# One attention-block backward loop: dO pass in two PSUM banks, dH of Q apart, tail work moved behind pass and fold

## The chip, the cores and the metric

The kernel runs on one core of one Trainium2 chip. The metric is the device time of one execution in microseconds, the median of several runs. A core has TensorE (matrix products and transposes into PSUM[...]), VectorE and ScalarE (both read PSUM and copy it to SBUF, which is called eviction here), GpSimd[...] and SyncE, which here only issues DMAs. Each engine works its instructions in program order and waits on semaphores.

## The reference, cut to what matters

The reference returns a forward pass and the gradients of all its inputs. The forward pass is an attention block with a recurrent memory, then a gated MLP, each behind a modulated layer norm. In the attention block the 2048 rows are 64 segments of 32. Each segment is worked together with 8 memory rows, and its first 8 output rows are the memory of the next segment:

```python
for s in range(n_seg):                                     # 64 segments
    xs = x[:, s * seg_len:(s + 1) * seg_len, :].copy()     # 32 rows
    h = jnp.concatenate([mem, xs], axis=1)                 # 40 rows of 512
    q = jnp.einsum('btd,dhe->bhte', h, Wq)                 # 32 heads of 128
    k = jnp.einsum('btd,dhe->bhte', h, Wk)
    v = jnp.einsum('btd,dhe->bhte', h, Wv)
    scores = jnp.einsum('bhqe,bhke->bhqk', q, k) * scale
    scores = jnp.where(mask[None, None], scores, -1000000000.0)
    p = _softmax(scores, axis=-1)
    o = jnp.einsum('bhqk,bhke->bhqe', p, v)
    o = jnp.einsum('bhte,hed->btd', o, Wo)
    mem = o[:, :M, :].copy()
    outs.append(o[:, M:, :])
...
_out, _vjp = jax.vjp(_f, A_x, A_mem0, A_Wq, A_Wk, A_Wv, A_Wo, B_w_gate, B_w_up, B_w_down, c, w_mod)
_grads = _vjp(grad_out)
```

Backward, the segments run from the last to the first. A step takes the gradient dy of the segment's output (32 rows of which the 8 of the memory come from the step just done), and forms dO = dy Wo^T, dV, dS, dK, dQ per head, and dH = dV Wv^T + dK Wk^T + dQ Wq^T, the gradient of the 40 rows. The 8 memory rows of dH are needed before the next step's dO pass can begin: this is the recurrence.

## The kernel before: the parts that the change touches

Products with few rows use TensorE as four column tiles: a stationary operand of 32 columns fills one tile, and four matmuls with different tiles run side by side. A result of 512 columns thus stands in one bank as four partial rows of 32, which are added up by a "fold": the sum is split into a bf16 high part and a bf16 low part, and short matmuls with a selecting matrix (`foldsel`) add the four quarters and turn them at once.

```python
    row = pool.tile([1, 128], F32, name="modrow", bufs=1)
    nc.scalar.activation(row[:], ps[0:1, :], AF.Copy)
    nc.gpsimd.dma_start(self.MODROW[:, sl], row[:])

return load, products
...

    j = n % 4
    self.nc.tensor.matmul(ps[32 * j:32 * j + 32, :], lhsT=lhsT, rhs=w, start=(n < 4), stop=(n >= total - 4),
                          tile_position=(0, 32 * j))

def pair_mm(self, ps, x, w, n, total):

    nc = self.nc
...
def col_pass(self, psp, w, hf, lhs, rows, eng):

    E, DC = self.cfg.E, self.cfg.DC
    ps = psp.tile([128, 512], F32, name="pass_ps", tag="p")
    for c in range(DC):
        wc = w[:, c, :].rearrange("p (h e) -> p h e", e=E)
        for j in range(4):
            rhs = wc[:, 12 * hf + j:12 * hf + j + 10:3, :] if j < 3 else wc[:, 24 + 4 * hf:28 + 4 * hf, :]
            self.nc.tensor.matmul(ps[32 * j:32 * j + 32, :], lhsT=lhs(c), rhs=rhs, start=(c == 0), stop=(c == DC - 1),
                                  tile_position=(0, 32 * j))
    if eng is None:
        return ps
    self.evac(eng, rows[:, 512 * hf:512 * hf + 512], ps[:])
...
def fold_split(self, pool, ps, name, tags=""):

    nc = self.nc
    parts = []
    for h in range(2):
        sl = slice(256 * h, 256 * h + 256)
        hi = pool.tile([128, 256], BF16, name=name + "_hi", tag=f"{tags}hi{h}", bufs=1)
        nc.scalar.activation(hi[:], ps[:, sl], AF.Copy)
        parts.append(hi)
    for h in range(2):
        lo = pool.tile([128, 256], BF16, name=name + "_lo", tag=f"{tags}lo{h}", bufs=1)
        nc.vector.tensor_tensor(lo[:], ps[:, 256 * h:256 * h + 256], parts[h][:], op=ALU.subtract)
        parts.append(lo)
    return parts

def fold_sum(self, psp, parts, name, tag):

    ft = psp.tile([128, self.cfg.DC, 32], F32, name=name + "_ft", tag=tag)
    for c in range(self.cfg.DC):
        for i in range(2):
            self.nc.tensor.matmul(ft[:, c, :], lhsT=parts[2 * i + c // 2][:, (c % 2) * 128:(c % 2) * 128 + 128],
                                  rhs=self.foldsel[:], start=(i == 0), stop=(i == 1))
    return ft
...
def store_rows(self, psp, pool, ft, dram, name, tag, then=None):

    nc = self.nc
    tb = pool.tile([128, 128], BF16, name=name + "_tb")
    nc.vector.tensor_copy(tb[:], ft[:].rearrange("p c r -> p (c r)"))

    def f():
        tp = psp.tile([128, 128], BF16, name=name + "_tp", tag=tag)
        nc.tensor.transpose(tp[:], tb[:], self.ident[:])
        rb = pool.tile([128, 128], BF16, name=name + "_rb")
        nc.vector.tensor_copy(rb[:], tp[:])
        nc.gpsimd.dma_start(dram, rb[:])
        if then is not None:
            then(rb)

    self.later.append(f)
```

`pair_mm` puts two heads side by side in such a bank: two column tiles take the left, two the right half of the 512 columns, so its result is 256 wide and folds with `foldhalf`. The forward pass uses it; the backward loop does not. In the loop (`NS` = 64 steps, `G` = 11 groups of three heads, 128 columns each, worked in `NP` = 3 parts of 4, 4 and 3 groups) the pools and the parts concerned are:

```python
rxp = ctx.enter_context(tc.tile_pool(name="p4rx", bufs=3, reuse_waits="tile"))
sb2 = ctx.enter_context(tc.tile_pool(name="p4s2", bufs=2, reuse_waits="tile"))
psp = ctx.enter_context(tc.tile_pool(name="p4ps", bufs=6, space=PSUM, reuse_waits="tile"))
psb = ctx.enter_context(tc.tile_pool(name="p4psb", bufs=1, space=PSUM, reuse_waits="tile"))
...
def turn(hf):
    for k, eng in enumerate(("act", "dve")):
        tp = psp.tile([128, 2, 128], BF16, name="turn_ps", tag="p")
        i0 = 4 * hf + 2 * k
        for i in range(2):
            nc.tensor.transpose(tp[:, i, :], RAd[:, (i0 + i) * 128:(i0 + i + 1) * 128], self.ident[:, :])
        to_heads(eng, tp[:], i0, 2, 0, 32, 0)
...
def proj_b(t, hf):
    ps = self.col_pass(psp, WoT, hf, lambda c: dbs[t][:, c, :, :].rearrange("p s q -> p (s q)"), None, None)
    return lambda: self.evac(("act", "dve")[hf], RBds[t % 2][:, 512 * hf:512 * hf + 512], ps[:])
...
def grad_out(nm, xt, pi, eng, ps):
    self.evac(eng, part3(xt, pi), ps[:, 0:min(PG, G - pi * PG), :])
    if pi == NP - 1:
        rows = rxp.tile([128, G, 128], BF16, name="rows_x")
        nc.sync.dma_start(rows[:], xt[:, :], transpose=True)
        dram = {"dVT": self.DVR, "dKT": self.DKR, "dQT": self.DQR}[nm][s]
        row_stores.append(lambda: nc.gpsimd.dma_start(dram, rows[:]))
...
def dht(X, WT, pi):
    if dh_ps[0] is None:
        dh_ps[0] = psb.tile([128, 512], F32, name="dh_ps", tag="dh")
    for h in range(pi * PG * 3, min(H, (pi + 1) * PG * 3)):
        off = (h // 3) * GW + (h % 3) * 32
        self.col_mm(dh_ps[0], X[:, off:off + 32], WT[:, h, :], n_dh[0], 3 * H)
        n_dh[0] += 1

for hf in range(2):
    self.col_pass(psp, WoT, hf, lambda c: dyT[:, c, :], RAd, ("dve", "act")[hf])
    nc.gpsimd.tensor_copy(dOst[0:96, 512 * hf:512 * hf + 512], RAd[0:96, 512 * hf:512 * hf + 512])
if pend:
    pend.pop()()
store_rows_x(1)
if s == 0:
    self.p5_first()
turn(0)
turn(1)
gv0 = grad_mm("dVT", dOst, Pst, 0)
prod(0)
dp(0)
prod(1)
dp(1)
prod(2)
dp(2)
gv1 = grad_mm("dVT", dOst, Pst, 1)
grad_out("dVT", dVT, 0, "act", gv0)
dost(2)
grad_out("dVT", dVT, 1, "act", gv1)
ds(0)
ds(1)
ds(2)
self.pop_later()
dht(dVT, WvT, 0)
dht(dVT, WvT, 1)
if s > 0:
    to_heads("pool", btd[:], 0, 8, 32, 8, 8 * ((s - 1) % nseg_t))
if s4 == 3 and s > 3:
    get_db(s // 4 - 1)
store_rows_x(0)
if s == 0:
    self.p5_second()
for pi in range(NP):
    dstt(pi)
gks = [grad_mm("dKT", Qst, dS, pi) for pi in range(NP)]
load_rows(Qst_t, self.QST, s - 1)
gv2 = grad_mm("dVT", dOst, Pst, 2)
if s > 0:
    dO_tails(s - 1)
for pi in range(NP):
    grad_out("dKT", dKT, pi, "dve", gks[pi])
grad_out("dVT", dVT, 2, "act", gv2)
self.pop_later()
for pi in range(NP):
    grad_part("dQT", Kst, dST, dQT, pi, "act")
split = tail.split()
load_rows(Kst_t, self.KST, s - 1)
for pi in range(NP):
    dht(dKT, WkT, pi)
dht(dVT, WvT, 2)
if split:
    self.pop_later()
for pi in range(NP):
    dht(dQT, WqT, pi)
parts = self.fold_split(sb2, dh_ps[0], "dh")
tail.collect(s % nseg_t, [dVT, dKT, dQT])
tail.chunk()
ft = self.fold_sum(psp, parts, "dh", "p")
if dyT_next is not None:
    nc.scalar.activation(dyT_next[:, :, 0:M], ft[:, :, 0:M], AF.Copy)
if s > 3:
    if s4 >= 2:
        proj_b(s // 4 - 1, 3 - s4)()
    elif s4 == 1:
        turn_b(s // 4 - 1)()
...
pend.append(lambda ft=ft, s=s, then=then: self.store_rows(psp, sb2, ft, self.DHA[s], "dh", "p", then))
if s4 == 0:
    tail.begin(s, [WvT, WkT, WqT])
```

`turn` transposes dO per head pair and copies it into dOT, which the dp products read; `proj_b` and `turn_b` do the dO pass and its turning for the memory rows of the next group of four segments. The tail (`TailRows`) gathers the last 8 rows of dV, dK and dQ over four segments (`collect`) and forms their dH once a group: 96 matmuls with 32 stationary columns in four pieces of 24, one piece a step (`chunk`); then `split` makes high and low part of the sum, and its fold runs when `pop_later` is next called. `row_stores` hands the turned rows of dK, dV and dQ to GpSimd's DMA queue in that order.

## Time and profile before

| what | value |
|---|---|
| time, median of 3 runs | 3183.44 us (3178.51 to 3185.88) |
| span of the profiled run | 3180.4 us, mean granted TensorE clock 0.983 |
| TensorE, weight load | 2985.1 us (94%), 1729.6 us (54%) |
| VectorE, ScalarE, GpSimd | 1579.3 us (50%), 1161.1 us (37%), 1481.1 us (47%) |
| DMA moved | 726.12 MB, mean 228 GB/s |
| backward loop: first dO pass to the last one | 1570.8 to 2555.5 us |

The profile names an instruction by its engine, its line in the kernel (a helper's line where a helper records it) and by tiles, output left of the arrow. A square bracket holds the idle time of the engine before it and what ended it. PE is TensorE's matmul side, PEld its loading of stationary operands, DVE VectorE, ACT ScalarE, POOL GpSimd and SP SyncE. TensorE's matmuls are pipelined and their ends are modelled, so distances between starts are safer than durations. A busy share over the whole span says little here, as the program has several phases; the loop is read by itself.

### The profile page before, as it was taken

The numbers are of one execution on the slowest core, as the hardware profiler recorded it, in microseconds if no ns is written. First come the engines' busy times: TensorE is split into PE (matmuls) and PEld (weight loads), VectorE is DVE, ScalarE is ACT, GpSimd is POOL, SyncE is SP. The second block draws the span as 40 slices with busy tenths as digits, with TensorE's granted clock in tenths as the row PEclk, the third lists the DMA queues.
The fourth block names the chain that finished last, engine by engine and source line by source line (L and its number), as shares of the span: only waits on it lengthen the run. The fifth ranks groups of instructions, "written<-read, shape, count | busy, mean of one in ns | idle before, by whom it ended". The sixth has DMA issues, their size and how long they took to land.

```text
span 3180.4 us, 98869 instructions
## 1 busy us (share of the span) xinstructions
PE 2985.1 (94%) x40069; PEld 1729.6 (54%) x40069; DVE 1579.3 (50%) x3770; ACT 1161.1 (37%) x2829; POOL 1481.1 (47%) x2973
## 2 busy tenths in 40 slices
PE   5999999999998899989999999999999969999999
PEld 3666666666665444445555555555555534445454
DVE  4655666666654777642245455554554521332221
ACT  2454454454454433322244444444444410100011
POOL 3666666666664466521244444444444421233322
PEclk8999999999999899999999999999999989999999
DMA  8788888889888798897599999999999999998886
GB/s 291 206 208 208 202 201 207 198 206 212 198 206 236 182 221 219 209 294 245 171 260 255 265 256 263 268 274 263 263 261 251 261 226 223 231 213 192 204 231 152
DMA packets 958892, 726.12 MB, mean 228 GB/s; under 512 B 656018, under 2 KB 831138, under 8 KB 958308
## 3 DMA queue, kind: packets, MB, share of 16 engines
q1 hardware_dynamic: 827940, 508.77, 71.1%
q0 software_dynamic: 59056, 148.62, 13.9%
q10 hardware_dynamic: 71440, 62.40, 7.8%
q8 instruction: 316, 5.18, 0.7%
q14 instruction: 140, 1.15, 0.1%
HBM read 294.91 MB, written 276.33 MB: 180 GB/s over the span
## 4 chain that ended last, share of the span: by engine, by line
PE 34%; DMA 9%; issue 8%; ACT 3%; POOL 2%; DVE 2%; SPq 1%; ACTq 0%; POOLq 0%; DVEq 0%
PE dh_ps L212 10%; PE gps L1820 5%; PE pass_ps L249 4%; PE g_ps L1509 4%; PE dh_tps L212 2%; DMA rows<-DKR 2%; PE gps5o L1833 2%; PE tps L1424 2%; PE dp_ps L1488 1%; DMA rows<-DQR 1%; PE dp_ps L1496 1%; ACT RAd L61 1%; DMA rows<-OSR 1%; PE dh_ft L318 1%; PE turn_ps L1390 1%
## 5 line engine op out<-in xcount | busy, mean ns | idle before, releaser
L1820 PE MATMUL gps<-rows,hrows 128*128 128x512 bf16 (+2 forms) x2160 | 417.8, 355 | 4.5 <-ACT ot L61 3.1
L1820 PEld LDWEIGHTS <-hrows 128*128 128x128 bf16 x2160 | 211.1, 98 | 209.4 <-issue 5.1
L249 PEld LDWEIGHTS <-hT 128*32 128x32 bf16 x6144 | 158.2, 97 | 161.3 <-issue 1.9
L1538 POOL COPY dOst<-RAd 96x512 bf16<-96x512 bf16 x128 | 78.6, 614 | 356.4 <-DVE RAd L63 345.0
L852 POOL TENSOR_TENSOR Pst<-Pst,rden 120x1408 bf16<-120x1408 bf16 x63 | 161.2, 2559 | 114.7 <-issue 81.5
L1824 POOL DMA_DIRECT2D out_dram<-ot x108 | 81.5, 755 | 232.9 <-DVE ot L63 138.9
L63 DVE CAST ot<-gps 128x512 bf16<-128x512 f32 (+3 forms) x76 | 47.9, 633 | 254.0 <-PE gps L1820 122.5
L309 DVE TENSOR_TENSOR dh_lo<-dh_ps,dh_hi 128x256 bf16<-128x256 f32 x128 | 48.4, 420 | 240.2 <-ACT dh_hi L305 240.2
L1833 PE MATMUL gps5o<-WoT,rows 128*128 128x512 bf16 x600 | 134.3, 387 | 26.6 <-DMA rows<-OSR 26.6
L61 ACT ACTIVATE ot<-gps 128x512 bf16<-128x512 f32 (+3 forms) x75 | 41.2, 549 | 281.4 <-PE gps L1820 128.7
L212 PE MATMUL dh_ps<-WvT,dVT 128*32 128x512 bf16 x2048 | 136.1, 385 | 0.0
L249 PE MATMUL pass_ps<-Wv,hT 128*32 128x512 bf16 x2048 | 133.5, 380 | 0.0
L1498 DVE SCALAR_TENSOR_TENSOR dS<-dp_ps,Pst_l 128x512 bf16<-128x512 f32 (+1 forms) x192 | 112.2, 640 | 35.0 <-PE dp_ps L1496 34.9
L249 PE MATMUL pass_ps<-WoT,dyT 128*32 128x512 bf16 x2048 | 122.9, 382 | 5.2 <-ACT dyT L1597 5.2
L220 PE MATMUL at_ps<-Wo,OT 128*32 128x256 bf16 x4096 | 124.7, 275 | 0.5 <-DVE OT L63 0.2
L249 PE MATMUL pass_ps<-Wk,hT 128*32 128x512 bf16 x2048 | 123.6, 383 | 1.5 <-ACT hT L842 1.1
L63 DVE CAST RA0v<-pass_ps 128x512 bf16<-128x512 f32 x128 | 88.4, 690 | 70.5 <-PE pass_ps L249 68.1
L212 PE MATMUL dh_ps<-WkT,dKT 128*32 128x512 bf16 x2048 | 122.4, 380 | 0.0
L212 PE MATMUL dh_ps<-WqT,dQT 128*32 128x512 bf16 x2048 | 121.9, 379 | 0.0
L249 PE MATMUL pass_ps<-Wq,hT 128*32 128x512 bf16 x2048 | 121.8, 379 | 0.0
L61 ACT ACTIVATE dVT<-g_ps 128x512 bf16<-128x512 f32 (+1 forms) x192 | 108.1, 563 | 36.6 <-PE g_ps L1509 20.5
L694 ACT ACTIVATE ET<-st_ps 128x480 bf16<-128x480 f32 (+1 forms) x192 | 96.2, 537 | 53.7 <-ACT qT L61 37.0
(411 smaller groups left out, 7035.9 us busy)
## 6 DMA issues: line engine op xcount, KB each, us to landing
OSR<-Ost SPq DMA_DIRECT2D x64, 352.0 KB
OT<-OT SPq DMA_DIRECT2D x64, 352.0 KB
VT<-VTr SPq DMA_DIRECT2D x64, 352.0 KB
PS<-Pst SPq DMA_DIRECT2D x64, 352.0 KB
OT_l<-OT SPq DMA_DIRECT2D x64, 352.0 KB
Pst_l<-PS SPq DMA_DIRECT2D x64, 352.0 KB
VT_l<-VT SPq DMA_DIRECT2D x64, 352.0 KB
DKR<-rows_x POOLq DMA_DIRECT2D x64, 352.0 KB, 5.8
```

The costliest lines, as they stand in the source:

```text
L61: return nc.scalar.activation(out, in_, AF.Copy)
L63: return nc.vector.tensor_copy(out, in_)
L212: self.nc.tensor.matmul(ps[32 * j:32 * j + 32, :], lhsT=lhsT, rhs=w, start=(n < 4), stop=(n >= total - 4), tile_position=(0, 32 * j))
L220: nc.tensor.matmul(ps[32 * j:32 * j + 32, :], lhsT=x[k], rhs=w[k][:, 256 * d:256 * d + 256], start=(n == 0), stop=(n == total - 1), tile_p ...
L249: self.nc.tensor.matmul(ps[32 * j:32 * j + 32, :], lhsT=lhs(c), rhs=rhs, start=(c == 0), stop=(c == DC - 1), tile_position=(0, 32 * j))
L694: nc.scalar.activation(part3(ET, pi)[:, 0:n, 0:120], st_ps[:, 0:n, 0:120], AF.Exp, scale=cfg.scale)
L852: nc.gpsimd.tensor_tensor(Pst[0:120, :, :], Pst[0:120, :, :], rden[:, :].unsqueeze(2).to_broadcast([120, G, 128]), op=ALU.mult)
L1498: nc.vector.scalar_tensor_tensor(out=part3(dS, pi), in0=ps[:, 0:n, :], scalar=cfg.scale, in1=part3(Pst, pi), op0=ALU.mult, op1=ALU.mult)
L1509: nc.tensor.matmul(ps[:, j, :], lhsT=lh[:, g * GW:(g + 1) * GW], rhs=rh[:, g * GW:(g + 1) * GW], start=True, stop=True)
L1820: nc.tensor.matmul(ps[:, 0:ng * E], lhsT=hrows[:, tp_, c * 128:(c + 1) * 128], rhs=rows[:, tp_, 0:ng * E], start=(tp_ == 0), stop=(tp_ == ...
L1824: nc.gpsimd.dma_start(outw[c * 128:(c + 1) * 128, h0:h0 + 3 * (ng - 1) + 1:3, :], ot[:, 0:ng * E].rearrange("p (h e) -> p h e", e=E))
L1833: nc.tensor.matmul(pss[gg][:], lhsT=rows[:, tp_, gg * E:(gg + 1) * E], rhs=dyrows[:, tp_, :], start=(tp_ == order[0]), stop=(tp_ == order[ ...
```

## The change

It reorders the hand-over between two steps of the backward loop and gives some of its results a place of their own:

- the dO pass of a step goes in three pieces (heads groups of 4, 2 and 2 in each column tile) instead of two; the last two have a bank each and are evicted apart by ScalarE;
- dH of V and K alone goes into the bank `dh_ps` and is split while TensorE does dH of Q, which is formed in pairs in a bank of its own; the fold adds both;
- high and low part are 512 wide and live in dST and dS, which are free by then;
- the tail's 96 matmuls go in seven pieces, some behind the dO pass and one behind the fold; its own fold moves next to the step's fold; the memory rows' dO pass uses the bank of `dh_ps`, and half of each of its halves stands behind the fold, the other half behind the next dO pass;
- the transpose of dV into rows is issued in two parts, eight groups early and three late.

It is meant to give TensorE work where it waits for an eviction, and to start one transpose earlier. Cut to its core:

```diff
-    def col_pass(self, psp, w, hf, lhs, rows, eng):
+    def col_pass(self, psp, w, hf, lhs, rows, eng, ps=None, cs=None, steps=None):
 
         E, DC = self.cfg.E, self.cfg.DC
-        ps = psp.tile([128, 512], F32, name="pass_ps", tag="p")
-        for c in range(DC):
+        a, n = steps or (4 * hf, 4)
+        if ps is None:
+            ps = psp.tile([128, n * E], F32, name="pass_ps", tag="p")
+        for c in cs or range(DC):
             wc = w[:, c, :].rearrange("p (h e) -> p h e", e=E)
             for j in range(4):
-                rhs = wc[:, 12 * hf + j:12 * hf + j + 10:3, :] if j < 3 else wc[:, 24 + 4 * hf:28 + 4 * hf, :]
+                rhs = wc[:, 3 * a + j:3 * (a + n - 1) + j + 1:3, :] if j < 3 else wc[:, 24 + a:24 + a + n, :]
                 self.nc.tensor.matmul(ps[32 * j:32 * j + 32, :], lhsT=lhs(c), rhs=rhs, start=(c == 0), stop=(c == DC - 1),
                                       tile_position=(0, 32 * j))
         if eng is None:
             return ps
-        self.evac(eng, rows[:, 512 * hf:512 * hf + 512], ps[:])
+        self.evac(eng, rows[:, a * E:(a + n) * E], ps[:])
...
-    def fold_split(self, pool, ps, name, tags=""):
+    def fold_split(self, pool, ps, name, home=None):
 
         nc = self.nc
...
+        hi, lo = (pool.tile([128, 512], BF16, name=f"{name}_{x}", tag=x, bufs=1)[:, :] if home is None
+                  else home[:, 512 * i:512 * i + 512] for i, x in enumerate(("hi", "lo")))
+        nc.scalar.activation(hi, ps[:], AF.Copy)
+        nc.vector.tensor_tensor(lo, ps[:], hi, op=ALU.subtract)
+        return hi, lo
+
+    def fold_sum(self, psp, parts, name, tag, pair=()):
 
         ft = psp.tile([128, self.cfg.DC, 32], F32, name=name + "_ft", tag=tag)
-        for c in range(self.cfg.DC):
-            for i in range(2):
-                self.nc.tensor.matmul(ft[:, c, :], lhsT=parts[2 * i + c // 2][:, (c % 2) * 128:(c % 2) * 128 + 128],
-                                      rhs=self.foldsel[:], start=(i == 0), stop=(i == 1))
+        cs = range(self.cfg.DC)
+        mms = [(t[:, c * 128:(c + 1) * 128], self.foldsel[:], c) for t in parts for c in cs]
+        mms += [(t[:, (c % 2) * 128:(c % 2) * 128 + 128], self.foldhalf[:, c // 2, :], c) for t in pair for c in cs]
+        for n, (lhsT, rhs, c) in enumerate(mms):
+            self.nc.tensor.matmul(ft[:, c, :], lhsT=lhsT, rhs=rhs, start=(n == 0), stop=(n >= len(mms) - self.cfg.DC),
+                                  skip_group_check=True)
         return ft
...
-def proj_b(t, hf):
-    ps = self.col_pass(psp, WoT, hf, lambda c: dbs[t][:, c, :, :].rearrange("p s q -> p (s q)"), None, None)
-    return lambda: self.evac(("act", "dve")[hf], RBds[t % 2][:, 512 * hf:512 * hf + 512], ps[:])
+def proj_b(t, hf, parts=1):
+    ps = psb.tile([128, 512], F32, name="pass_ps", tag="dh")
+
+    def part(k):
+        self.col_pass(psp, WoT, hf, lambda c: dbs[t][:, c, :, :].rearrange("p s q -> p (s q)"), None, None, ps,
+                      range(k * DC // parts, (k + 1) * DC // parts))
+
+    part(0)
+
+    def rest():
+        for k in range(1, parts):
+            part(k)
+        return lambda: self.evac(("act", "dve")[hf], RBds[t % 2][:, 512 * hf:512 * hf + 512], ps[:])
+
+    return rest
...
-tail = TailRows(self, sb2, psp, psb, 3, "dh", self.DHB, 4)
+b_rest = []
+tail = TailRows(self, sb2, psp, psb, 3, "dh", self.DHB, (16, 24, 8, 8, 16, 8, 16), home=dSs[0])
...
+        early = 2 * PG if nm == "dVT" else 0
+        if pi == 1 and early:
+            turned[nm] = rxp.tile([128, G, 128], BF16, name="rows_x")
+            nc.sync.dma_start(turned[nm][:, 0:early, :], xt[:, 0:early * GW], transpose=True)
         if pi == NP - 1:
-            rows = rxp.tile([128, G, 128], BF16, name="rows_x")
-            nc.sync.dma_start(rows[:], xt[:, :], transpose=True)
+            rows = turned.get(nm) or rxp.tile([128, G, 128], BF16, name="rows_x")
+            nc.sync.dma_start(rows[:, early:G, :], xt[:, early * GW:G * GW], transpose=True)
             dram = {"dVT": self.DVR, "dKT": self.DKR, "dQT": self.DQR}[nm][s]
             row_stores.append(lambda: nc.gpsimd.dma_start(dram, rows[:]))
...
-            self.col_mm(dh_ps[0], X[:, off:off + 32], WT[:, h, :], n_dh[0], 3 * H)
+            self.col_mm(dh_ps[0], X[:, off:off + 32], WT[:, h, :], n_dh[0], 2 * H)
             n_dh[0] += 1
 
+    def dht_pairs(X, WT):
+        ps = psp.tile([128, 256], F32, name="dhq_ps", tag="p")
+        off = lambda h: (h // 3) * GW + (h % 3) * 32
+        for n in range(H // 2):
+            hs = (2 * n, 2 * n + 1)
+            self.pair_mm(ps, [X[:, off(h):off(h) + 32] for h in hs], [WT[:, h, :] for h in hs], n, H // 2)
+        return ps
+
+    for a, n, eng in ((0, 4, "dve"), (4, 2, "act"), (6, 2, "act")):
+        self.col_pass(psp, WoT, 0, lambda c: dyT[:, c, :], RAd, eng, steps=(a, n))
     for hf in range(2):
-        self.col_pass(psp, WoT, hf, lambda c: dyT[:, c, :], RAd, ("dve", "act")[hf])
         nc.gpsimd.tensor_copy(dOst[0:96, 512 * hf:512 * hf + 512], RAd[0:96, 512 * hf:512 * hf + 512])
-    if pend:
-        pend.pop()()
+    b_done = b_rest.pop()() if b_rest else None
+    if s4 < 2:
+        tail.chunk()
     store_rows_x(1)
     if s == 0:
         self.p5_first()
...
     grad_out("dVT", dVT, 0, "act", gv0)
+    if b_done:
+        b_done()
     dost(2)
     grad_out("dVT", dVT, 1, "act", gv1)
...
+    parts = self.fold_split(sb2, dh_ps[0], "dh", dST)
+    pair = self.split_pair(sb2, dht_pairs(dQT, WqT), "dh")
+    tail.collect(s % nseg_t, [dVT, dKT, dQT])
+    tail.chunk()
     if split:
         self.pop_later()
-    for pi in range(NP):
-        dht(dQT, WqT, pi)
-    parts = self.fold_split(sb2, dh_ps[0], "dh")
-    tail.collect(s % nseg_t, [dVT, dKT, dQT])
-    tail.chunk()
-    ft = self.fold_sum(psp, parts, "dh", "p")
+    ft = self.fold_sum(psp, parts, "dh", "p", pair)
     if dyT_next is not None:
         nc.scalar.activation(dyT_next[:, :, 0:M], ft[:, :, 0:M], AF.Copy)
-    if s > 3:
-        if s4 >= 2:
-            proj_b(s // 4 - 1, 3 - s4)()
-        elif s4 == 1:
-            turn_b(s // 4 - 1)()
+    g = s // 4
+    if s >= NS - 2:
+        proj_b(g - 1, 3 - s4)()()
+    elif s4 == 3 and g > 0:
+        b_rest.append(proj_b(g - 1, 1, 2))
+    elif s4 == 2:
+        tail.chunk()
+    elif s4 == 1 and g > 0:
+        turn_b(g - 1)()
+    elif s4 == 0 and g > 1:
+        b_rest.append(proj_b(g - 2, 0, 2))
...
-    pend.append(lambda ft=ft, s=s, then=then: self.store_rows(psp, sb2, ft, self.DHA[s], "dh", "p", then))
+    self.store_rows(psp, sb2, ft, self.DHA[s], "dh", "p", then)
     if s4 == 0:
         tail.begin(s, [WvT, WkT, WqT])
-pend.pop()()
```

## The prediction

> **What bounds the kernel now.** I read the slices of the span first, then busy time by stretch, then the order of TensorE's instructions inside one step of the backward loop, then the waits. The change touches only that loop: 64 steps, whose first dO pass starts at 1570.8 us and whose last stretch ends at about 2570 us, one third of the span. In the middle of it:
>
> ```profile
> core 0: us, PE busy (x) PEld busy (x) DVE busy (x) ACT busy (x) POOL busy (x), PEclk, DMA share, GB/s
> 2000.00:2150.00 150.00, 144.35 (x2442) 86.62 (x2439) 77.70 (x210) 68.93 (x177) 70.25 (x174) 1.00 1.13 269
> ```
>
> TensorE is busy 96% of the time at full clock, and VectorE, ScalarE and GpSimd about half. So the loop is a chain of TensorE work with small holes, and only filling holes or shedding instructions can help. The DMA share of 1.13 says that the queues are never empty either; I return to that. The timeline of TensorE shows where the holes are. These lines are the end of step s=27, the whole hand-over, and the start of s=26:
>
> ```profile
> 2145.75 0.60 PE L212 MATMUL dh_ps<-WvT,dVT 128*32 128x512 bf16 x8
> 2146.28 0.19 PE L318 MATMUL dh_b_ft<-foldsel,dh_b_hi 128*128 128x32 bf16 x1
> ...
> 2146.99 1.91 PE L212 MATMUL dh_ps<-WqT,dQT 128*32 128x512 bf16 x32
> 2148.72 1.47 PE L212 MATMUL dh_tps<-WvT,dh_tail 128*32 128x512 bf16 x24
> 2150.12 0.19 PE L318 MATMUL dh_ft<-foldsel,dh_hi 128*128 128x32 bf16 x1
> ...
> 2150.24 0.18 PE L318 MATMUL dh_ft<-foldsel,dh_hi 128*128 128x32 bf16 x1
> 2150.45 0.19 PE L318 MATMUL dh_ft<-foldsel,dh_lo 128*128 128x32 bf16 x1
> ...
> 2150.62 1.05 PE L249 MATMUL pass_ps<-WoT,dyb 128*32 128x512 bf16 x16
> 2151.50 1.90 PE L249 MATMUL pass_ps<-WoT,dyT 128*32 128x512 bf16 x32
> 2153.40 0.40 PE L1390 MATMUL turn_ps<-ident,RAd 128*128 128x128 bf16 x4
> 2154.16 0.40 PE L1390 MATMUL turn_ps<-ident,RAd 128*128 128x128 bf16 x4 [0.36 <-ACT RAd L61]
> 2154.40 0.39 PE L1509 MATMUL g_ps<-Pst_l,dOst 128*128 128x128 bf16 x4
> ```
>
> Ends are modelled, so I read distances between starts. Three holes. (1) Four transposes cost 0.22 us (2154.16 to 2154.40, nearly), but the second four begin 0.76 us after the first: 0.54 us is lost to the 512-wide eviction of the second dO half. (2) The fold's matmuls follow each other at 0.03 us, but one step takes 0.21 (2150.24 to 2150.45): the last low part is not there yet, 0.18 us. The tail's fold, a group of its own, takes 0.71 us (2146.28 to 2146.99) for eight such matmuls. (3) Every fourth step has nothing between the fold and the next dO pass:
>
> ```profile
> 2134.97 0.18 PE L318 MATMUL dh_ft<-foldsel,dh_lo 128*128 128x32 bf16 x1
> 2135.43 1.91 PE L249 MATMUL pass_ps<-WoT,dyT 128*32 128x512 bf16 x32 [0.29 <-ACT dyT L1597]
> ```
>
> 0.46 us, against 0.10 where the dO rows of the memory stand between (2150.52, the last fold matmul, to 2150.62). The dO pass starts of this group of four, from the same timeline, are 2135.43, 2151.50, 2166.97, 2181.79 and 2196.53: steps of 16.07, 15.47, 14.82 and 14.74, together 61.1 us. Most groups repeat these to 0.01 us; a few steps are 1 to 4 us longer, so that the mean step is (2555.5 - 1593.8)/62 = 15.51 us against 15.28 without them. The longer ones go with DMA waits, for example
>
> ```profile
> PE g_ps L1509 <- DMA dOst<-RBd: 4.5, 2, 2.7
> PE g_ps L1509 <- DMA Kst<-KST: 3.1, 3, 1.6
> ACT dVT L61 <- DMA rows_x<-dVT: 7.1, 10, 2.4
> q1 hardware_dynamic: 283235, 157.90, 91.3%
> q0 software_dynamic: 20685, 64.47, 20.9%
> ```
>
> (us in all, times, longest; then packets, MB and share of 16 engines, all within 1700 to 2560.)
>
> **What the Trainium skill says.** "TensorEngine Tiling (Array Packing)", section Key Properties: changing the tiling mode drains TensorE. The trace agrees: 24 tail matmuls, in six quads of 0.217 us (32 take 1.74), should take 1.30; the fold, in full-array mode, starts 1.40 after them. So a change of mode costs about 0.1 us each way, and the place of each filler matters. "PSUM — Partial Sum Buffer", section "PSUM bank collisions raise a hardware error": reads and matmul writes must be kept apart by bank and quadrant. This is why splitting an eviction early needs a second bank; in the trace ScalarE starts the half at 2153.51, after all its 16 matmuls. "ScalarE: Activation LUTs", Rules for kernel authors: about 0.3 us plus 0.83 ns an element. The trace has 0.60 us for 512 and 0.38 for 256: the slope is right (0.86), the fixed part is 0.16, and I use the trace. "DMA: Bandwidth & Descriptors", section "Issuing engines are not separate DMA queues": all issuers end on the same 16 engines. The two shares above add to over 100%, so a later transpose is paid by something.
>
> **The change part by part.**
>
> *Second dO half in two banks, filler behind the pass.* Heads 4-5 and 6-7 get 16 matmuls of 256 columns each and evictions of 0.38 us, and 8 column matmuls (0.43 us) of tail or of the memory's dO stand between the pass and the turns. Counted from where the turns began before: the last eviction starts at +0.11 and ends at +0.50; the turns start at +0.43 and reach the last pair at +0.76. That hole closes. But the eight turns now come in one run, and the copies behind them do not shrink: VectorE started its first copy 0.44 after the turns began (2153.84 against 2153.40) and three of them took 0.42, so it is done at 0.43 + 0.44 + 0.42 = 1.29 and dp(0) can start at about 1.36, where TensorE would be ready at 0.43 + 0.45 + 0.22 = 1.10. So about 0.25 comes back as a wait for dOT; before, dp began at 1.22 (2154.62). Net: 0.43 us of work done for 0.14 us, plus some 0.05 us of smaller waits there now: I take 0.35 us a step, 64 x 0.35 = 22 us.
>
> *Narrow matmuls.* The forward pass has the pair form: 64 of 256 columns start at 700.42 and what follows starts at 702.18, 1.76 us, against 1.74 for 32 of 512. So dH of Q in pairs and the half pass cost about 0.03 us a step: 2 us.
>
> *dH of Q in a bank of its own.* V and K are split into high and low (one 512-wide eviction and subtraction) under the 1.76 us of Q. Only a 256-wide pair then stands between Q and the fold: high 0.38, low 0.42, with starts about 0.2 after the matmuls' end, ready at some 1.1 to 1.2. Before it stand 16 tail matmuls (0.87), a drain (0.1) and eight fold matmuls of V and K (0.22), so the low part is just in time. The 0.18 hole goes, but eight more fold matmuls at 0.03 come in: minus 0.04 a step, a loss of 2.5 us.
>
> *Tail's fold moved.* It stood alone between V and Q (0.71 us and a drain of 0.1). It now follows the tail chunk, next to the other fold, its parts long ready: 0.22. Once in four steps, 16 x 0.59 = 9.4 us.
>
> *A filler behind every fold.* The uncovered 0.36 us goes once in four steps: 5.8 us. The tail's 96 matmuls (16, 24, 8, 8, 16, 8, 16) and the memory's 32 a group are otherwise the same, only elsewhere.
>
> *The memory's dO shares the bank of dH.* Its eviction must end before dV's dH begins. In one step of four it is VectorE's (0.69 us), queued behind the copies and products: I let TensorE wait 0.2 there, 3 us in all.
>
> *dV in two parts.* One more transpose a step (eight groups, then three). It removes ScalarE's wait for the old dV to be read (7.1 us in 55 steps, of which TensorE felt about 2). But row buffers rotate: the early part is now the first of the step to want one, and waits until the last step's dV rows are stored. I read that from the order of both programs: before, dK came first and waited for DKR, which is stored earlier. DVR is issued at 2155.28 and takes a median 7.6 us, so the early part starts near 2162.5, where dK started at 2160.78; then come the load of Q, dK, the late dV and dQ on the same in-order queue, about 1 us later than now. I set 5 us against the gain for longer DMA waits.
>
> Sum: 22 - 2 - 2.5 + 9.4 + 5.8 - 3 + 2 - 5 = about 27 us, on 3183: 3156. A regular group of four would take about 59.2 us instead of 61.1 (30 us of the sum stand in it).
>
> **The rivals.** *Copies of dOT take the place of the eviction wholly*: for it speaks that ScalarE and VectorE copy back to back from 2153.84 to 2154.95 already; against it, that dp(1) and dp(2) need the last copies only 0.2 and 0.4 us later. The 22 us would shrink to about 8: 3170. *DMA becomes the bound*: the loop of DVR store (7.6), early dV, load of Q, dK, late dV (2 + 0.4 + 2.6 + 1 us of issue, from the durations of these instructions now) and the 3 to 4 us until a transpose lands makes 16.6 to 17.6 us, more than the 15 of a step. Against it: a good part of these latencies is queueing, which shrinks when the issue comes later, and queue 1 still has some 9% to spare. If it binds, the step stays at 15.5 to 16 and the time goes to 3180 to 3215. *More than 2% gained* would need 64 us: all holes named above together make 64 x 0.72 + 16 x (0.36 + 0.6) = 61 us without any cost, so this I hold almost excluded, unless the long steps vanish (15 us) as well.
>
> **Range and chances.** The regular part is sure to 8 us or so; dOT copies can cost 14 of it, DMA 30 to 50. Eight in ten: 3132 to 3190. Faster by over 2%: 0.04; within 2%: 0.91; slower by over 2%: 0.05.
>
> **What would show it.** Right: the eight turns in one run, no wait for RAd, a hole of about 0.25 us before dp; fold matmuls at 0.03 us throughout; groups of four near 59.2 us. Wrong: the wait for dOT at 0.5 us; a hole before the high and low parts of Q; long steps more frequent than one in five, with waits for rows_x, dOst, Kst or Qst; VectorE's late eviction of the memory's dO ahead of dS, so that the transposes of dS wait.

## The result, and the profile after

The changed kernel takes 3233.01 us (median of 4 runs, 3230.39 to 3240.46); the kernel before, timed beside it, 3183.27 us (3178.51 to 3185.88). The ratio is 1.0162, with a 95% interval of 1.0141 to 1.0182: the change made the kernel 50 us slower, where the prediction had 27 us of gain and a range that ended at 3190.

The profiled run has a span of 3231.8 us and a mean granted TensorE clock of 0.977 (before: 3180.4 and 0.983). From the first dO pass of the backward loop to its last, the trace has 1577.4 to 2605.5 us: 1028.1 us instead of 984.7. That is 43 of the 51 us by which the spans differ. The part ahead of the loop is 6.6 us longer. Kernels that are alike there differ by as much in their profiles (first dO pass at 1572.1 us in e14_idle, 1577.9 in e1_whole, 1585.4 in e12_halves, all below), so I don't put this piece down to the change.

The chain that ended last, by engine, from the page of the changed kernel:

```profile
PE 35%; DMA 14%; issue 5%; POOL 2%; SPq 1%; DVE 1%; ACT 0%; POOLq 0%; ACTq 0%; DVEq 0%
```

Before, this line had DMA at 9%. Busy time in the stretch that the prediction used, for the changed kernel (columns: length, busy time and count of each engine, granted clock, DMA share, GB/s):

```profile
core 0: us, PE busy (x) PEld busy (x) DVE busy (x) ACT busy (x) POOL busy (x), PEclk, DMA share, GB/s
2000.00:2150.00 150.00, 136.92 (x2792) 94.61 (x2788) 73.65 (x190) 67.12 (x169) 64.91 (x161) 0.97 1.10 253
```

TensorE fell from 144.35 us busy to 136.92, and its clock from 1.00 to 0.97. The other engines do less in the same time too. The DMA share stays above 1 (1.13 before), and the bytes per second fall from 269 to 253. The timeline of TensorE in the changed kernel shows the hand-over to step s=37 and its products (start, duration, engine, line, operation, tiles, count, and idle time before it with its releaser):

```profile
2003.81 0.36 PE L316 MATMUL dh_ft<-foldsel,dST 128*128 128x32 bf16 x8
2004.03 0.25 PE L316 MATMUL dh_ft<-foldsel,dh_hi 128*128 128x32 bf16 x4
2004.12 0.25 PE L316 MATMUL dh_ft<-foldsel,dh_lo 128*128 128x32 bf16 x4
2004.31 0.61 PE L212 MATMUL dh_tps<-WkT,dh_tail 128*32 128x512 bf16 x8
2004.75 1.91 PE L251 MATMUL pass_ps<-WoT,dyT 128*32 128x512 bf16 x48
2006.48 0.61 PE L212 MATMUL dh_tps<-WkT,dh_tail 128*32 128x512 bf16 x8
2007.02 0.62 PE L1388 MATMUL turn_ps<-ident,RAd 128*128 128x128 bf16 x8
2007.48 0.39 PE L1521 MATMUL g_ps<-Pst_l,dOst 128*128 128x128 bf16 x4
2007.73 0.96 PE L1500 MATMUL dp_ps<-VT_l,dOT 128*128 128x128 bf16 x11
...
2012.33 0.33 PE L1521 MATMUL g_ps<-Pst_l,dOst 128*128 128x128 bf16 x3
2014.83 1.13 PE L1521 MATMUL g_ps<-dST,Kst 128*128 128x128 bf16 x11 [2.17 <-DMA Kst<-KST]
2015.89 3.19 PE L212 MATMUL dh_ps<-WkT,dKT 128*32 128x512 bf16 x32
2018.91 0.60 PE L212 MATMUL dh_ps<-WvT,dVT 128*32 128x512 bf16 x8
```

All that the prediction wanted of TensorE is there. The eight turns stand in one run (2007.02 to 2007.48, 0.058 us each), the fold has no break (16 matmuls from 2003.81 to 2004.31), and a filler stands behind the fold and behind the pass. The loss comes after that: TensorE stops 2.17 us for K's rows, which the products of dQ need, and the 32 matmuls that follow take 3.02 us (2015.89 to 2018.91), where they take 1.74 at full speed.

Waits of TensorE in the changed kernel, 1700 to 2590 us (us in all, times, longest):

```profile
PE g_ps L1521 <- DMA Kst<-KST: 55.8, 35, 4.1
PE g_ps L1521 <- DMA dOst<-RBd: 9.9, 8, 2.3
```

These two were 3.1 and 4.5 us before. What the queue of loads and transposes (SyncE's) waits for in the same stretch, first line only, L1530 being the early part of dV:

```profile
SPq L1530 <- DMA DKR<-rows_x: 235.1, 55, 7.4
```

And SyncE's queue in the same step as above (duration is that of the issue):

```profile
2009.64 0.52 SPq L1439 DMA_DIRECT2D Kst<-KST  x1
2010.21 0.39 SPq L1422 DMA_DIRECT2D OT_l<-OT  x1
2010.65 0.52 SPq L1422 DMA_DIRECT2D Pst_l<-PS  x1
2011.21 0.49 SPq L1425 DMA_DIRECT2D VT_l<-VT  x1
2013.85 1.90 SPq L1530 DMA_TRANSPOSE rows_x<-dVT  x1
2015.79 0.87 SPq L1439 DMA_DIRECT2D Qst<-QST  x1
2018.73 3.29 SPq L1533 DMA_TRANSPOSE rows_x<-dKT  x1
2022.12 1.20 SPq L1533 DMA_TRANSPOSE rows_x<-dVT  x1
2023.43 1.91 SPq L1533 DMA_TRANSPOSE rows_x<-dQT  x1
```

The load of K starts at 2009.64, 4.9 us into the step (the dO pass began at 2004.75), and its rows are wanted at 2012.66. The queue is in order: K's load stands behind the transposes of the step before, and these stand behind that step's early part of dV. How such a part holds up the queue can be seen at 2013.85: 2.2 us pass between the end of the load of V (2011.70) and the early part, and all that follows it, the next load of K too, is later by them. The medians over the loop (whole steps within 1696 to 2540 us, worked out from the trace; each time counted from the start of the step's dO pass) show the shift:

| us from the dO pass | before: issued, landed | after: issued, landed |
|---|---|---|
| load of K | 2.19, 6.52 | 4.54, 9.15 |
| store of dK rows | 3.24, 9.37 | 5.31, 11.23 |
| load of Q | 7.90, 14.46 | 12.73, 18.81 |
| transpose of dK | 9.60, 17.18 | 13.86, 20.65 |
| first product of dQ on TensorE | 7.87 | 9.18 |
| mean step | 15.58 | 16.17 |

The load of K lost the 1.3 us of slack that it had, and now lands with its reader.

A second view separates what TensorE does from where it is stopped. Every step has a floor, the undisturbed time of its kind (s mod 4 = 3, 2, 1, 0). In the kernel before most steps repeat it. In the changed kernel only 13 of 59 come within 0.3 us of it; its four values are taken from e8_after_plain below, where the same TensorE work repeats them in most steps. What the steps have above their floors, summed over the 59 steps behind the first four, is the excess:

| kernel | floors of the four kinds | their sum | steps over 0.3 us above | excess |
|---|---|---|---|---|
| before | 16.07, 15.47, 14.82, 14.73 | 61.09 | 10 of 59 | 15.2 us |
| after | 14.48, 15.00, 14.29, 14.29 | 58.06 | 46 of 59 | 98.9 us |

The floor of the changed kernel is *lower* than predicted (59.2), and the excess eats it more than once. In the same 59 steps the gaps of over 0.15 us between TensorE's matmuls make 75 us, 58.5 of them in front of K, and it ran 37 us at half clock, half of which, 19, is lost (last section): together 94 of the 98.9 us. The experiments ask why K is late, and what else is.

### The profile page after: what moved, and what is told of

The parts are those of the page before. It is cut to its first block, busy times and chain, and to the rows that moved or that the text cites. A ratio compares the mean times of both kernels' runs of the same rounds, so it can differ in the third digit from the quotient of the medians.

```text
span 3231.8 us, 105823 instructions
## 1 busy us (share of the span) xinstructions
PE 2992.2 (93%) x43577; PEld 1823.8 (56%) x43653; DVE 1600.9 (50%) x3738; ACT 1188.7 (37%) x2861; POOL 1477.3 (46%) x2973
## 4 chain that ended last, share of the span: by engine, by line
PE 35%; DMA 14%; issue 5%; POOL 2%; SPq 1%; DVE 1%; ACT 0%; POOLq 0%; ACTq 0%; DVEq 0%
PE dh_ps L212 6%; DMA Kst<-KST 5%; PE gps L1854 4%; PE pass_ps L251 4%; PE dhq_ps L220 3%; PE gps L1209 3%; PE gps5o L1867 3%; PE g_ps L1521 3%; PE dh_tps L212 2%; DMA dOst<-RBd 2%; DMA rows<-DKR 2%; DMA rows<-OSR 1%; PE dp_ps L1500 1%; PE turn_ps L1388 1%; POOL out_dram L1858 1%
## 5 line engine op out<-in xcount | busy, mean ns | idle before, releaser
L306 DVE TENSOR_TENSOR dST<-dh_ps,dST 128x512 bf16<-128x512 f32 x64 | 44.3, 692 | 195.7 <-ACT dST L305 195.7
L212 PE MATMUL dh_ps<-WkT,dKT 128*32 128x512 bf16 x2048 | 134.7, 409 | 0.0
L251 PE MATMUL pass_ps<-WoT,dyT 128*32 128x256 bf16 (+1 forms) x3072 | 123.5, 308 | 1.8 <-PE pass_ps L251 0.8
L220 PE MATMUL dhq_ps<-WqT,dQT 128*32 128x256 bf16 x4096 | 123.6, 273 | 0.5 <-issue 0.3
L220 PEld LDWEIGHTS <-dQT 128*32 128x32 bf16 x4096 | 109.5, 97 | 18.9 <-issue 3.9
```

Of the source, the lines that this page charges most:

```text
L220: nc.tensor.matmul(ps[32 * j:32 * j + 32, :], lhsT=x[k], rhs=w[k][:, 256 * d:256 * d + 256], start=(n == 0), stop=(n == total - 1), tile_p ...
```

## The experiments

Two theories. **Ring**: the early part of dV takes the first row buffer that comes free. It waits for dK's store, behind it wait the load of Q and the transpose of dK, and dK's store waits for that. By the medians above this closes in one step: the store lands at 11.23, early dV is issued at 11.29, Q at 12.73 and dK at 13.86, dK lands at 20.65, which is 4.5 of the next step, and the store is issued at 5.31. That GpSimd's queue has to wait for turned rows ahead of this store, in 45 of 52 steps, is in its waits as well (1696 to 2540 us; which of the two transposes came last is inferred):

```profile
POOL DKR L1535 <- DMA rows_x<-dVT: 60.8, 26, 4.8
POOL DKR L1535 <- DMA rows_x<-dKT: 44.5, 19, 3.4
```

**Load**: the 16 DMA engines are full with this work whatever its order, so that a faster TensorE just runs into them.

### The change without the split of dV (e1_whole)

```diff
-                    early = 2 * PG if nm == "dVT" else 0
+                    early = 0
```

> The changed kernel with dV turned whole again, all else kept. Ring theory (the early part of dV waits for the stored dK rows of the step before, which makes a ring of transposes and stores of about 16 us a step): the ring is gone, the dK rows wait for their buffer as in the kernel before, TensorE's step falls to about 14.9 us, time 3140 to 3160. Rival A (the rearranged TensorE work itself costs the time: narrow matmuls, shared bank, more fold matmuls): stays at 3220 to 3235. Rival B (a faster TensorE meets a DMA that is full whatever the order): 3180 to 3200.

Measured: 3198.46 us (3184.72 to 3211.80), ratio 1.0036 (1.0021 to 1.0052). This lies in the range of rival B, the load theory, and 38 us above that of the ring. The split costs 35 us by the medians (3233.01 - 3198.46), 40 by the two ratios to the kernel before, and what is left of the change still loses 11 us (0.36%), where 27 and more were to be gained. Against the floors of after the excess is 74.6 us. Of it 51 us fall in the steps with s mod 4 = 3, where the floor is 14.48: all but the last of the 15 take 15.83 us or more. Waits of TensorE, 1696 to 2540 us:

```profile
PE pass_ps L251 <- issue: 14.6, 9, 3.1
PE g_ps L1521 <- DMA Kst<-KST: 8.4, 9, 2.1
PE dh_tp L328 <- ACT dVT L61: 6.0, 11, 1.1
PE g_ps L1521 <- DMA dOst<-RBd: 5.6, 6, 1.8
```

With the order of before (K's load issued at 2.74, landed at 7.49) the wait for K falls to 8.4 us, so order explains most of that wait. But other stops are there, shorter and spread; of these only the one for the memory's dO was there before in this size (4.5 us). The ring alone is not the answer.

### The split alone (e2_split)

The kernel before, with dV's transpose in two parts and nothing else:

```diff
+                    early = 2 * PG if nm == "dVT" else 0
+                    if pi == 1 and early:
+                        turned[nm] = rxp.tile([128, G, 128], BF16, name="rows_x")
+                        nc.sync.dma_start(turned[nm][:, 0:early, :], xt[:, 0:early * GW], transpose=True)
                     if pi == NP - 1:
-                        rows = rxp.tile([128, G, 128], BF16, name="rows_x")
-                        nc.sync.dma_start(rows[:], xt[:, :], transpose=True)
+                        rows = turned.get(nm) or rxp.tile([128, G, 128], BF16, name="rows_x")
+                        nc.sync.dma_start(rows[:, early:G, :], xt[:, early * GW:G * GW], transpose=True)
```

> The kernel before with only dV turned in two parts. Ring theory: the same ring of 16 us stands here, so the step goes from 15.5 to about 16.1 and the time to 3210 to 3235, with TensorE waiting for Kst. Rivals A and B: no change, 3175 to 3190, as the old step of 15.5 us is slow enough.

Measured: 3225.00 us (3220.94 to 3230.17), ratio 1.0119 (1.0082 to 1.0155). By the medians the split costs 38 us here (the kernel before, timed beside it, took 3186.90) and 35 us in the changed kernel: it is a cost of its own, beside the old order of TensorE's work as beside the new. This is the range of the ring theory. TensorE waits in e2_split, 1696 to 2540 us:

```profile
PE g_ps L1509 <- DMA Kst<-KST: 33.2, 22, 3.3
```

It waits for K, as in the changed kernel.

### Breaking the ring with a fourth row buffer (e3_four)

The changed kernel with four row buffers. For room, high and low part of Q's dH go into unused columns of dST and dS, and one small buffer of the tail goes.

```diff
-            rxp = ctx.enter_context(tc.tile_pool(name="p4rx", bufs=3, reuse_waits="tile"))
+            rxp = ctx.enter_context(tc.tile_pool(name="p4rx", bufs=4, reuse_waits="tile"))
...
-                pair = self.split_pair(sb2, dht_pairs(dQT, WqT), "dh")
+                dhq = dht_pairs(dQT, WqT)
+                pair = dST[:, 1024:1280], dS[:, 1024:1280]
```

> The changed kernel with four row buffers instead of three (the parts of Q's dH live in dST and dS to make room). Ring theory: the early part of dV finds a free buffer, no wait of 4 us for DKR on the sync queue, time 3140 to 3165. Rival C (the split is dear because there are more transposes, each with its own cost on the queue and the DMA engines, whatever the buffers): 3200 to 3235.

Measured: 3253.42 us (3245.22 to 3256.49), ratio 1.0203 (1.0166 to 1.0240): slower than both theories said. Waits of TensorE, 1696 to 2540 us:

```profile
PE pass_ps L251 <- issue: 36.3, 19, 4.7
PE g_ps L1521 <- DMA dOst<-RBd: 20.4, 10, 3.9
PE g_ps L1521 <- DMA Kst<-KST: 2.3, 4, 1.0
```

The early part no longer waits for a buffer (issued at a median 6.59 us into the step, where it was 11.29), and the wait for K is all but gone. But the same time and more is lost in the dO pass, in stops that no semaphore explains, and at the small loads of the memory's dO. The queue is freed and its transposes reach the DMA engines earlier, and the time is lost elsewhere; the share of the hardware queue, which carries loads and transposes, is 93.9% here, the highest of all kernels. The changes made for room are not what costs: e16_whole4 below has them too and is no slower than e1_whole.

### The load of K ahead of the transposes (e4_kst)

The changed kernel, with the transposes of dK, of dV's late part and of dQ issued behind the load of the next K (`to_turn` has collected them where they were issued before):

```diff
                 load_rows(Kst_t, self.KST, s - 1)
+                for x in to_turn:
+                    turn_rows(*x)
```

> The changed kernel with the transposes of dK and late dV issued behind the load of the next K, so that the load of K leaves the end of the queue. Ring theory: the wait for Kst goes, but the ring of early dV, dK, store of dK is as long as before, so the step stays near 16 us and TensorE waits elsewhere (the eviction of dK or dV for its old rows): 3200 to 3240. Rival D (only the place of the load of K in the queue hurts): 3145 to 3165.

Measured: 3267.09 us (3261.22 to 3274.53), ratio 1.0251 (1.0211 to 1.0291). Waits of TensorE, 1696 to 2540 us:

```profile
PE g_ps L1521 <- DMA dOst<-RBd: 52.0, 17, 6.8
PE g_ps L1521 <- DVE dKT L63: 15.2, 13, 2.7
```

Both theories had less (3240 at most). The wait for K is gone, and a longer one for the memory's dO is in its place; the mean step is 16.98 us. The ring stands here: the early part still waits for dK's store, 202.3 us in 50 steps. Taking this one wait away only moved it.

### The same bytes without the transpose (e8_after_plain, e9_before_plain)

Both kernels with every transpose of dV, dK and dQ replaced by a plain copy of as many bytes between the same tiles. The rows are then not turned, so what is formed from them isn't the gradient; TensorE's work in the loop is untouched. The early part of dV and the kernel before are changed in the same way as here:

```diff
-                        nc.sync.dma_start(rows[:, early:G, :], xt[:, early * GW:G * GW], transpose=True)
+                        nc.sync.dma_start(rows[:, early:G, :], gl3(xt)[:, early:G, :])
```

> The changed kernel with every transpose of dV, dK and dQ replaced by a plain copy of the same bytes between the same buffers (the rows stored are not turned, so what is made of them is wrong; the waits and buffers are the same). If DMA is what took the gain: no waits for Kst, regular steps of 14.3 to 15.0 us throughout, time 3115 to 3145. If TensorE's rearrangement itself costs: 3170 or more, and no better than the kernel before with the same replacement.

> The kernel before with the same replacement of transposes by plain copies. DMA theory: it had only some 15 us of irregular steps to lose, so 3160 to 3178, and the changed kernel with the replacement is 30 to 45 us below it. Rival: both within 10 us of each other.

Measured: after with plain copies 3120.05 us (3116.82 to 3121.34), ratio to before 0.9799 (0.9780 to 0.9819); before with plain copies 3158.03 us (3149.20 to 3161.23), 0.9914 (0.9886 to 0.9943). Both are as the DMA theory had them, e9 being 2 us below its range. This pair is the verdict on the TensorE part: **the change is worth 38 us where the transposes do not press**. The floors are those of the table above in both; the excess falls to 6.6 us and to none (-0.3).

It also shows the price of the transposes: 3183.27 - 3158.03 = 25 us in the kernel before, 3233.01 - 3120.05 = 113 us in the changed one. The 88 us between them, less the 38 us gained, are the 50 us by which the change lost. The hardware queue, 1700 to 2540 us (packets, MB, share of 16 engines): before, after, after with plain copies, before with plain copies.

```profile
q1 hardware_dynamic: 277566, 154.90, 91.3%
```

```profile
q1 hardware_dynamic: 267354, 148.64, 91.6%
```

```profile
q1 hardware_dynamic: 85299, 163.16, 67.8%
```

```profile
q1 hardware_dynamic: 69266, 157.94, 59.9%
```

The transposes move in packets of 256 bytes, the copies of whole rows in packets of 2816; with plain copies the queue moves a little more and takes a third less time. In the kernel before this is (0.913 - 0.599) x 15.58 = 4.9 us of all 16 engines in each step, if the packets' time is taken as work of an engine (it may hold some waiting of theirs). The Trainium skill, "Advanced Engine Details and Errata", section "X-Bar Transpose (TRN2)", says that transposing DMAs are as fast as regular ones. For the load they put on the engines beside other traffic, the runs here say otherwise, and they decide.

The waits of the ring's kind are in e8_after_plain as well. What SyncE's queue waits for, 1696 to 2540 us:

```profile
SPq L1530 <- DMA DKR<-rows_x: 403.1, 55, 8.5
```

The early part waits 7.3 us a step for the buffer, longer than in the changed kernel (4.3), and TensorE does not feel it. So this wait is no measure of what it costs. Nor does the ring close here: dK's copy lands 1.5 us into the next step, its store is issued at 3.04, the place that GpSimd's program gives it, and GpSimd waits for copied rows ahead of it in 6 of 57 steps. This pair therefore takes away both, the load and the closed ring, and doesn't tell them apart; e1_whole does, and e15_dqsplit below.

### dV turned ahead of dK, whole (e7_dvfirst, e6_dvfirst_kst)

The split did two things: it made one transpose more, and put a transpose of dV ahead of that of dK. e7 is e1_whole with the order alone; e6 adds the load of K between the two.

```diff
+                grad_out("dVT", dVT, 2, "act", gv2)
                 for pi in range(NP):
                     grad_out("dKT", dKT, pi, "dve", gks[pi])
-                grad_out("dVT", dVT, 2, "act", gv2)
```

> The changed kernel with dV turned whole but ahead of dK (dV is evicted first). Theory: the old dV rows are read before the next eviction of dV, the 6 us of waiting for that go, and no ring is closed, since the store of dV follows a transpose that ends sooner: 5 to 15 us less than with dV whole behind dK, 3180 to 3195. Rival (the DMA engines have no room, whatever the order): as dV whole, 3195 to 3202.

> As the one with dV ahead, with the load of the next K between the turns of dV and dK. Theory: Kst lands several us before its use, its 8 us of waits go, dK's turn is about 1 us later and its store still in time: 3165 to 3190. Rival: the later dK closes the ring again (turn of dK, store, buffer) or the late store of dQ holds up the dO rows: 3200 or more.

Measured: e7 3234.18 us (3226.35 to 3238.24), ratio 1.0157 (1.0133 to 1.0181); e6 3241.83 us (3219.26 to 3250.45), ratio 1.0173 (1.0129 to 1.0216). Waits of TensorE in e7, 1696 to 2540 us:

```profile
PE g_ps L1521 <- DMA dOst<-RBd: 32.1, 14, 5.2
PE g_ps L1521 <- DMA Kst<-KST: 22.2, 17, 3.3
```

The order alone costs 36 us over e1_whole by the medians, as much as the split. For e7 both theories had less; for e6 the rival's 3200 or more came. An additional transpose is thus not needed for a loss of this size, but that the same cause is at work in the split is not shown: e7 turns dV later than the split does. *Why* this order is so much worse these runs do not settle. The medians say only what comes late: in e7 dK's rows are stored by 12.76 us of the step (8.76 in e1_whole) and the memory's dO lands at 17.99 (15.76). e6 takes the wait for K away and is no faster, its wait for the memory's dO being 49.9 us instead of 32.1.

### dQ's rows from TensorE instead of a transpose (e10_dqrows), and its control (e14_idle)

If the transposes' load is the matter, one fewer should pay, even with TensorE doing more. e10 is e1_whole with dQ's rows formed by 11 more matmuls a step (dS^T times K), evicted by VectorE and stored at the step's end; as dQ needs no row buffer any more, there are two of them. e14 does the same matmuls and three evictions (384 columns each, two of them narrower than e10's 512), throws the result away and keeps the transpose and the three buffers.

```diff
+                for pi in range(NP):
+                    ps = grad_mm("dQ", dST, Kst, pi)
+                    n = min(PG, G - pi * PG)
+                    self.evac("dve", rows_q[:, pi * PG:pi * PG + n, :], ps[:, 0:n, :])
...
-                    if pi == NP - 1:
+                    if pi == NP - 1 and nm != "dQT":
```

> The changed kernel with dV turned whole, and the rows of dQ no longer turned by DMA: TensorE forms them itself (11 more matmuls of 0.056 us a step, dS^T with K, evicted by VectorE into a tile of their own, stored at the end of the step). DMA theory: TensorE's regular step grows by 0.65 to about 15.3 us, but a third of the transposes is gone and with it nearly all stalls: 3150 to 3175, below both kernels. Rival (only the ring of row buffers and the order matter, not the load on the DMA engines): the 0.65 us come on top of the time with dV whole, 3210 or more.

> Control of the run with dQ's rows from TensorE: the changed kernel with dV whole and the same 11 matmuls and evictions a step, but their result is thrown away and the DMA transposes of dQ stay. DMA theory (with dV whole, TensorE has run ahead of the DMA, so slower TensorE steps cost little): 0.65 us x 63 = 41 us more work, but 20 to 40 us fewer stalls: 3195 to 3220. Rival (the stalls have nothing to do with TensorE's pace): 3235 to 3245.

Measured: e10 3163.75 us (3158.26 to 3165.33), ratio 0.9931 (0.9908 to 0.9953), faster than both kernels; e14 3200.39 us (3191.09 to 3213.93), ratio 1.0061 (1.0045 to 1.0078). The floors of both are 15.29, 15.77, 15.11 and 15.11, together 61.28 and so 0.80 us a step above e1_whole's, 51 us in 64 steps. In e14 these 51 us of work cost 2 us by the medians and 8 by the ratios: the excess falls from 74.6 us to 35.0. TensorE was so far ahead of the DMA in e1_whole that work put into it was almost free. In e10, with the floors of e14, the excess is 2.5 us. Both are as the DMA theory had them. Busy time of e10 in the same stretch as above, and its hardware queue (1700 to 2540 us):

```profile
core 0: us, PE busy (x) PEld busy (x) DVE busy (x) ACT busy (x) POOL busy (x), PEclk, DMA share, GB/s
2000.00:2150.00 150.00, 149.75 (x3102) 107.45 (x3099) 97.45 (x240) 73.39 (x185) 69.79 (x174) 1.00 0.97 245
```

```profile
q1 hardware_dynamic: 203077, 137.23, 75.3%
```

TensorE is hardly stopped any more (gaps of 3 us in the 59 steps, 75 in the changed kernel). The DMA share is below 1 for the first time in a kernel that forms all rows, and the load of K is issued at 14.0 us of the step before, so that it no longer has to hurry.

### The split where the load is lighter (e15_dqsplit), and more buffers without it (e16_whole4, e17_dq3)

e15 is e10 with dV in two parts, e16 is e1_whole with four row buffers, and e17 is e10 with three instead of two (the edits of e3_four and e1_whole again).

```diff
-                    early = 0
+                    early = 2 * PG if nm == "dVT" else 0
```

> The kernel with dQ's rows from TensorE, and dV turned in two parts again. Load theory: with a third of the transposes gone the ring of early dV, dK and its store takes some 13 us and binds nothing, so no difference: 3155 to 3175. Ring theory in its strict form (the wait for the buffer costs whatever the load): 3190 or more.

> The changed kernel with dV whole and four row buffers. Ring theory: dV's turn waits for DKR or DVR no more, the ring through the store of dV (15.4 us a step with dV whole) opens, time 3155 to 3185. Load theory: more transposes are in the DMA queues at once, the fetch of TensorE's instructions and the small dO rows come later, so no gain or worse: 3200 to 3250.

> The kernel with dQ's rows from TensorE, with three row buffers for dV and dK instead of two. Nothing waits there for long now, so both theories expect the same time within 5 us: 3158 to 3168.

Measured: e15 3179.36 us (3171.33 to 3182.97), ratio 0.9992 (0.9980 to 1.0004); e16 3195.60 us (3189.12 to 3216.98), ratio 1.0050 (1.0027 to 1.0072); e17 3162.93 us (3161.06 to 3171.84), ratio 0.9947 (0.9929 to 0.9964). One more buffer gives nothing where dV is whole, with heavy load or light; for e16 neither range came, and no gain is what the load theory had. With one transpose fewer the split still costs 16 us (against e10 as against e17), half as much as under full load, more than the load theory has and less than the strict ring. The waits of TensorE and of SyncE's queue in e15, 1696 to 2540 us:

```profile
PE g_ps L1522 <- DMA Kst<-KST: 10.1, 11, 1.6
SPq L1531 <- DMA DKR<-rows_x: 350.7, 55, 8.4
```

The loop that the load theory put at 13 us closes here at the length of the step, 15.61 us. By the medians dK's store is issued at 5.90 us and lands at 12.37, early dV goes out at 12.39, the load of Q at 14.03 and dK at 14.27; dK lands at 20.56, which is 4.95 of the next step, and in all 54 steps GpSimd waits for turned rows ahead of the store. The load of K, issued at 14.0 us of the step before in e10, comes at 3.01 of its own, and TensorE waits for it. So the ring binds here, and makes K late; under full load it comes on top of a loss that is there without it (e1_whole).

### Two banks against one for the second dO half (e12_halves)

e1_whole with the second half in one bank again, the filler staying where it is.

```diff
-                for a, n, eng in ((0, 4, "dve"), (4, 2, "act"), (6, 2, "act")):
+                for a, n, eng in ((0, 4, "dve"), (4, 4, "act")):
```

> The changed kernel with dV whole and the dO pass in two halves of 512 columns again (the 8 matmuls behind the pass stay): 16 matmuls and 16 weight loads a step fewer. If the second bank is worth what was predicted for it beside the filler, the wait for RAd comes back by 0.1 to 0.2 us a step: regular steps 0.1 to 0.2 us longer. DMA theory: the time hardly moves, 3185 to 3205. Rival (the number of TensorE's instructions, whose fetch goes through the same DMA engines, makes the unexplained stops before the dO pass): fewer such stops, 3170 to 3185.

Measured: 3195.56 us (3180.92 to 3203.29), ratio 1.0033 (1.0020 to 1.0045), the same as e1_whole and as the DMA theory had it. In the floors the two banks are worth little (15.07 and 14.34 against 15.00 and 14.29 in two kinds of step, about 0.06 us, and nothing in a third): beside 0.43 us of filler nearly all of the 512-wide eviction is hidden anyway.

## Why the prediction was wrong

*Where the hole of the turns went, and the wait for dOT (part 1).* Right in mechanism: one run of turns, no wait for RAd. The wait for dOT came out smaller than the 0.25 us I set. In the timeline above, from the first product of dV to dp is 0.25 us where it was 0.22 before, and dp takes 0.80 us (2007.73 to 2008.53) where it took 0.71: 0.12 us more in all. That is a good part of why ordinary steps gained 0.44 to 0.53 us against the 0.28 that my terms make (0.35 - 0.03 - 0.04). The part named the second bank and the filler together; it is the filler that does it, the bank giving about 0.06 us beside it (e12_halves). The first rival, that dOT's copies take the eviction's place wholly, did not come.

*Narrow matmuls, dH of Q, fold of the tail, filler behind the fold, memory's dO (parts 2 to 6).* The fold has no 0.18 us break, as said. The kind s mod 4 = 3, which carries the moved tail fold and the filler, gained 16.07 - 14.48 = 1.59 us; these terms with the 0.2 for the memory's dO make 0.28 + 0.59 + 0.36 - 0.2 = 1.03. Together a group of four fell by 3.0 us, predicted 1.9. With plain copies in both kernels 38 us of this arrive in the time, where the prediction had 30 us in its steps. Single terms were not measured alone, only their sum.

*dV in two parts (part 7): this is the step that failed.* "I set 5 us against the gain for longer DMA waits" is the term. In its place the runs show 88 us, by which the transposes' price rose. The split makes 35 of these (e1_whole; 38 in e2_split), and some 53 come with the rest of the change. I read these 53 as TensorE being faster beside the same transposes: work put back into it without use takes away 40 of the 74.6 us of excess (e14_idle), and fewer instructions take away nothing (e12_halves). Both parts were missed, for two reasons.

First, the order of buffers. I wrote that the early part "waits until the last step's dV rows are stored". The trace has it waiting for dK's rows (DKR), not dV's: the buffer that comes free first. That it would be issued some 11 us into the step (2155.28 + 7.6 makes 2162.9, which is 11.4; measured 11.29) was right by luck: dK's rows landed at 9.37 before, and come at 11.23 only because the ring has pushed their store back. What I then misjudged is what stands behind it: the transpose of dK is issued 13.86 us into the step instead of 9.60, where I had "about 1 us later", and the delay reaches the next load of K.

Second, and larger, the rival that I set aside. The 91.3% of the hardware queue were read as "still some 9% to spare", and the latencies as "queueing, which shrinks when the issue comes later". The queue's share is 91.6% in the changed kernel, 91.1% in e1_whole, and still 91.8% in e14_idle, and what it moves in 840 us falls from 154.90 MB to 148.64: TensorE asked for shorter steps and the queue gave no more, so I take it as full. The latencies hardly shrank: the transpose of dK takes 7.31 us to land before and 6.59 after, the load of K 4.36 and 4.74. What could have been seen beforehand: two queues adding to 112% of the engines, and ten longer steps in 59, of which the plain copies leave two (e9_before_plain). Taking 0.75 us out of each step took away the slack in which late loads still came in time.

The rival "DMA becomes the bound" had 3180 to 3215 us, with a step of 15.5 to 16. It was right in kind: a loop of store, early dV, load of Q, dK and landing does bind, only through dK's store and not dV's, and it was set aside for reasons that did not hold (room in the queue, latencies that shrink). The measured step is 16.17 and the time 18 us above its range. It did not have TensorE's slow clock behind its stops, nor the loss that is there without any loop (e1_whole). A gain beyond 2%, the third rival, was never near.

*Signs named beforehand.* "Long steps more frequent than one in five, with waits for rows_x, dOst, Kst or Qst" is what came: 46 of 59 steps are more than 0.3 us above their floor, with waits for Kst and dOst. VectorE's late eviction of the memory's dO ahead of dS, also named, left no stop in the transposes of dS.

*What stays open.* Why a transpose of dV ahead of that of dK costs 36 us even when whole (e7_dvfirst); why the loss without the split gathers in one kind of step; and what the stops without a semaphore are (last section).

## What to carry to other kernels

Ahead of a change that makes the busiest engine faster, ask whether the DMA beside it could serve the shorter step. In this case the sum of the two main queues' shares told: in the four kernels where it is below 100% (e9 80.5, e8 89.6, e10 96.3, e17 97.2) the excess is -0.3 to 6.6 us; at 101% (e15) it is 14, and in the others, at 110 to 115%, 15 to 147. The kernel before stood at 112% with only ten long steps, and the gain of the change was returned as waits at whichever load was latest. Replacing the suspected transfers by plain copies of the same bytes in both kernels separates the two at once (38 us gained there, 50 us lost with the transposes). And where TensorE waits for DMA it can pay to form a second orientation by matmuls instead of a DMA transpose: here 0.80 us more floor a step brought the loop's excess from 74.6 us to 2.5.
